# Linear attention before a GELU MLP: 64-token blocks from wave 2 on, earlier first scores, half loads and a last block in three pieces

## The chip, the cores and the metric

The kernel runs on one core of a Trainium2 chip. Its engines each work through a queue of their own in order: TensorE (matrix products into PSUM), VectorE, ScalarE, GpSimd, and SyncE (SP), which here issues nearly all DMAs. The metric is the time of one execution on the device in microseconds, as the median of several runs. In the profile TensorE is PE (its weight loads PEld), VectorE DVE, ScalarE ACT and GpSimd POOL.

## The reference

Inputs are `q`, `k`, `v` with 4 batches, 8 heads, 768 tokens and 64 columns per head, a decay `lam` per head, and two weight matrices of 512x2048 and 2048x512.

```
for each block of 64 tokens, each batch and head:
    scores = (q k^T) * lam^(i-j) for i >= j, else 0
    out    = scores v + (q * lam^(i+1)) state
    state  = lam^64 state + (k * lam^(63-j))^T v
x = out as 3072 tokens x 512 columns
h = x w_in                       # 3072 x 2048
y = (h * sigmoid(1.702 h)) w_out # 3072 x 512
```

The recurrence over blocks gives the same result for any block length, up to rounding; with blocks of 128 the decay of the state is `lam^128`.

## The kernel before

The 3072 tokens are worked through in six **waves** of 512. Waves 0 and 1 take the first 256 tokens of two batches each, by functions whose names begin with `big_`; they are not changed. Waves 2 to 5 take the next 128 tokens of all four batches. The eight heads are four **pairs** p, two heads side by side on the 128 partitions. Each wave consists of attention, which makes `xT` (512 columns of x by 512 tokens, transposed), and of the MLP: 16 steps `mlp1` of four 512-column matmuls with a GELU on ScalarE (L413 to L423), then 16 steps `mlp2` of four matmuls, four steps to an output tile g of 128 tokens, which VectorE copies out of PSUM and SP stores (L428 to L439).

The attention of wave w + 1 is spread through the MLP of wave w. The order is written out by hand: `main` is the list of MLP steps, `side` a list of (position, call), and a call is issued ahead of the step of its position (L546 to L569). Every engine's queue follows this order. For waves 2 to 5 the calls are:

- `load` (L76): 24 DMAs on SP's queue, for a wave two ahead.
- `do_cast` (L204) for each pair: four VectorE products make `kqs`, k and q in bfloat16 with their decays; GpSimd casts v (`v_sb`); a DMA transpose on SP's queue turns `kqs` into `kqT`.
- `scores` (L358) for two pairs: q k^T of 128 tokens by 128 for each batch and head, 16 matmuls on half the rows of the array, and four VectorE passes that multiply by decay and causal mask (`sm`).
- `mix` (L390) for two pairs: 8 matmuls of the state `kv_sb` with q (L395) and 16 of `v_sb` with `sm` (L402) into `ps_o`, which ScalarE casts to `xT`. It can carry the `scores` of the next two pairs, and the states of all pairs behind the last `mix` of a wave: `state_mm` (L373) makes k^T v in PSUM, `state_up` (L383) is one VectorE operation per head, new = old * lam^128 + k^T v.

PSUM has eight banks: three ("mm") serve the MLP's sums, five ("att") the attention; `scores` inside `mix` borrows one of the three (`bank`, L220). A new tile takes the bank whose last use came first in program order, and its first matmul waits until that use is over. The constants (`consts`, `last_consts`, `late_mask`, `state_zeros`) are made at the start. The last output tile of all is computed in two halves of 256 columns (`mlp2_part`, L441).

Of the kernel before, what the change touches and what calls it, by code (L numbers as in the profile page):

```python
# [24 lines left out]
def kernel(  # L25
# [50 lines left out]
    def load(w):  # L76
        for g in range(2):
# [44 lines left out]
    mask_b, mask = const.tile([P, 2, 2, D], bf16, name="mask_b"), const.tile([P, 1, P], bf16, name="mask")  # L122
# [3 lines left out]
    blk_pow = const.tile([P, NP], f32, name="blk_pow")  # L126

    def consts(f0):
# [5 lines left out]
        nc.gpsimd.iota(i_k, pattern=[[0, 1]], base=P - 1, channel_multiplier=-1, **io)  # L134
        nc.gpsimd.iota(i_q, pattern=[[0, 1]], base=1, channel_multiplier=1, **io)
        nc.vector.memset(i_inv, -float(P))
        nc.vector.memset(i_blk, float(P))
# [20 lines left out]
    def last_consts():  # L158
        for h in range(2):
# [5 lines left out]
    def late_mask():  # L165
        nc.gpsimd.affine_select(mask, mask, pattern=[[0, 1], [1, P]], channel_multiplier=-1, base=0,
                                compare_op=mybir.AluOpType.is_ge, fill=0.0)

    def state_zeros():
        for p in range(NP):  # L170
            for i in range(2):
                nc.gpsimd.memset(kv_sb[i][p], 0.0)

    v_sb = [[const.tile([P, G, 2, D], bf16, name=f"v_sb{i}{p}") for p in range(NP)] for i in range(2)]
    kv_sb = [[const.tile([P, B, P], bf16, name=f"kv{i}{p}") for p in range(NP)] for i in range(2)]
    part_sb = [[const.tile([P, 2, BB, D], f32, name=f"part{i}{r}") for r in range(2)] for i in range(2)]
# [134 lines left out]
    def big_st(w, p0):  # L311
        first, second = part_sb[p0 // 2]
        for i in range(2):
            p = p0 + i
            nc.gpsimd.tensor_scalar(first[:, i], first[:, i], scalar1=blk_pow[:, p : p + 1], scalar2=None, op0=MUL)  # L315
# [41 lines left out]

    def scores(w, pairs, spare=False):  # L358
        s2 = {(p, h): bank([P, B, P], f32, "ps_s", spare and (p, h) == (pairs[-1], 1)) for p in pairs for h in range(2)}
        for p in pairs:  # L360
            kq = trans[w, p]
            for b in range(B):
                for h in range(2):
                    hs = slice(64 * h, 64 * h + 64)
                    nc.tensor.matmul(s2[p, h][:, b, :], kq[hs, 0, b, :], kq[hs, 1, b, :], start=True, stop=True)  # L365
        for p in pairs:
            for h in range(2):
                sm = work.tile([P, B, P], bf16, tag="sm", bufs=8, name="sm")
                nc.vector.scalar_tensor_tensor(sm, s2[p, h], inv_pow[:, 2 * p + h : 2 * p + h + 1],  # L369
                                               mask.to_broadcast([P, B, P]), op0=MUL, op1=MUL)  # L370
                masked[w, p, h] = sm

    def state_mm(w, pairs):  # L373
        ps_kv = bank([P, len(pairs), B, D], f32, "ps_kv")
        for i, p in enumerate(pairs):
            ks, vt = cast[w, p][:, 0], v_sb[w % 2][p]
            for b in range(B):
                for h in range(2):
                    hs = slice(64 * h, 64 * h + 64)
                    nc.tensor.matmul(ps_kv[hs, i, b, :], ks[:, b, hs], vt[:, b, h, :], start=True, stop=True)  # L380
        return ps_kv

    def state_up(w, pairs, ps_kv):  # L383
        for i, p in enumerate(pairs):
            for h in range(2):
                hs = slice(64 * h, 64 * h + 64)
# [213 lines left out]
```

## Time and profile before

| | |
|---|---|
| runs shown | 216.71, 211.70, 212.51 us; median 212.51 |
| profiled execution | 211.42 us, its span (first to last instruction) 209.7 |
| TensorE busy | 200.8 us, 96% of the span |
| VectorE, ScalarE, GpSimd busy | 93.1, 86.8, 44.9 us |
| granted TensorE clock | full in all slices |

The profile is of one execution. "Span" runs from the first to the last instruction; the execution's own time has some 1.7 us around it. A timeline row gives the start in us from the span's start, the length in us, the engine, the line and operation, the tiles and the count of instructions merged in the row; what stands in brackets is idle time ahead of it and what ended it. A matmul's length is from its start until its result stands in PSUM; matmuls overlap, so that the spacing of starts is much shorter than a length.

### The profile page before, as it was taken

Reading aid. Unit: us, or ns where it says so; the run is one execution under the profiler, and the core shown is the slowest. Engines: PE = TensorE matmul, PEld = TensorE weight load, DVE = VectorE, ACT = ScalarE, POOL = GpSimd, SP = SyncE. Lnnn points to the kernel's source line nnn. Section 1 sums busy time; section 2 is a strip of 40 time slices with the busy share of each in tenths; the row PEclk is TensorE's granted clock in tenths of the full one; section 3 lists DMA queues with packets and bytes.
Section 4 is the critical chain, followed back from the end, with each engine's and each line's share of the span. In section 5 each row is a group of like instructions: output and inputs, shape, how many; then the busy total and the mean of one; then the engine's idle time right before and its main releaser. Section 6 shows DMA issues by size and latency. Waiting matters only on the chain.

```text
span 209.7 us, 4312 instructions
## 1 busy us (share of the span) xinstructions
PE 200.8 (96%) x1719; PEld 105.1 (50%) x1747; DVE 93.1 (44%) x199; ACT 86.8 (41%) x160; POOL 44.9 (21%) x87
## 2 busy tenths in 40 slices
PE   7979999998999999999999999999999999999993
PEld 7654444464444456444545444545444545444462
DVE  3895000578840568915347905346915341100121
ACT  4658662346765022565202566202466202565000
POOL 3299950174871011200211001120000000000000
PEclk9999999999999999999999999999999999999999
DMA  6999999998799999998891599890570111100112
GB/s 173 276 207 205 206 204 220 299 270 194 175 254 261 182 226 189 299 190 199 198 247 63 152 188 222 196 248 3 149 152 0 52 51 50 53 0 0 50 54 96
DMA packets 88233, 33.83 MB, mean 161 GB/s; under 512 B 68630, under 2 KB 85270, under 8 KB 88214
## 3 DMA queue, kind: packets, MB, share of 16 engines
q1 hardware_dynamic: 83174, 28.98, 58.2%
q0 software_dynamic: 4224, 4.19, 12.4%
q10 hardware_dynamic: 816, 0.39, 0.6%
q8 instruction: 13, 0.21, 0.4%
q14 instruction: 6, 0.05, 0.1%
HBM read 27.26 MB, written 6.29 MB: 160 GB/s over the span
## 4 chain that ended last, share of the span: by engine, by line
PE 89%; DVE 6%; DMA 2%; issue 2%; SPq 0%; ACT 0%; DVEq 0%
PE ps_h L420 39%; PE ps_out L433 38%; DVE smb L279 3%; PE ps_o L402 2%; PE ps_s L365 2%; DVE kqb L241 2%; PE ps_o L395 2%; PE ps_part L444 2%; DMA kb<-in_k_dram 2%; PE ps_s L271 1%; PE ps_kv L380 1%; PE ps_o L338 1%; DVE xT L349 1%; PE ps_tk L258 1%; PE ps_tq L258 0%
## 5 line engine op out<-in xcount | busy, mean ns | idle before, releaser
L420 PE MATMUL ps_h<-xT,w_in 128*128 128x512 bf16 x375 | 84.2, 379 | 0.7 <-issue 0.2
L433 PE MATMUL ps_out<-w_out,g_sb 128*128 128x512 bf16 x352 | 80.4, 379 | 1.8 <-issue 1.4
L423 ACT ACTIVATE g_sb<-ps_h 128x512 bf16<-128x512 f32 x96 | 57.0, 597 | 44.1 <-PE ps_h L420 44.0
L420 PEld LDWEIGHTS <-w_in 128*128 128x128 bf16 x384 | 37.1, 98 | 44.7 <-issue 0.3
L433 PEld LDWEIGHTS <-g_sb 128*128 128x128 bf16 x368 | 35.0, 98 | 41.0
L437 DVE COPY o_sb<-ps_out 128x512 f32<-128x512 f32 x19 | 12.9, 690 | 51.0 <-PE ps_out L433 50.4
L369 DVE SCALAR_TENSOR_TENSOR sm<-ps_s,inv_pow,mask 128x512 bf16<-128x512 f32 x32 | 21.8, 742 | 22.7 <-PE ps_s L365 22.7
L407 ACT CAST xT<-ps_o 128x512 bf16<-128x512 f32 x16 | 8.6, 589 | 42.9 <-PE ps_o L402 36.2
L213 POOL CAST v_sb<-vf 128x512 bf16<-128x512 f32 x16 | 9.9, 624 | 71.4 <-DMA vf<-in_v_dram 62.3
L387 DVE SCALAR_TENSOR_TENSOR kv<-kv,blk_pow,ps_kv 64x256 bf16<-64x256 bf16 x24 | 11.5, 480 | 7.6 <-PE ps_kv L380 6.9
L241 DVE TENSOR_TENSOR kqb<-kb,kb_pow 128x256 bf16<-128x256 f32 x10 | 4.0, 422 | 22.4 <-DMA kb<-in_k_dram 20.2
L210 DVE TENSOR_SCALAR kqs<-kf,k_pow 128x256 bf16<-128x256 f32 x32 | 12.1, 379 | 1.8 <-DMA kf<-in_k_dram 1.6
L211 DVE TENSOR_SCALAR kqs<-qf,q_pow 128x256 bf16<-128x256 f32 x32 | 11.5, 358 | 1.4 <-DMA qf<-in_q_dram 1.4
L279 DVE SCALAR_TENSOR_TENSOR smb<-ps_s,inv_pow,mask_b 128x512 bf16<-128x512 f32 x16 | 11.0, 745 | 2.3 <-PE ps_s L271 2.3
L318 POOL TENSOR_TENSOR kv<-part,part 64x128 bf16<-64x128 f32 x16 | 7.3, 456 | 1.2
L229 PE MATMUL fill<-warm 128*128 128x64 bf16 (+2 forms) x61 | 5.6, 272 | 1.2 <-DVE warm L105 1.2
L229 PEld LDWEIGHTS <-warm 128*128 128x128 bf16 x79 | 5.5, 124 | 2.0 <-DVE warm L105 1.2
L315 POOL TENSOR_SCALAR part<-part,blk_pow 128x128 f32<-128x128 f32 x8 | 5.4, 673 | 3.5 <-ACT part L309 2.9
L241 DVE TENSOR_TENSOR kqb<-qb,qb_pow 128x256 bf16<-128x256 f32 x13 | 6.0, 497 | 0.0
L437 ACT COPY o_sb<-ps_out 128x512 f32<-128x512 f32 x4 | 2.3, 585 | 8.3 <-PE ps_out L433 8.3
L258 PEld LDWEIGHTS <-kqb 128*128 128x128 bf16 x64 | 4.4, 103 | 1.9 <-DVE kqb L241 0.4
L395 PEld LDWEIGHTS <-kv 128*128 128x128 bf16 x64 | 4.2, 98 | 1.9
(70 smaller groups left out, 111.5 us busy)
## 6 DMA issues: line engine op xcount, KB each, us to landing
out_dram<-o_sb SPq DMA_DIRECT2D x23, 256.0 KB, 2.6
kf<-in_k_dram SPq DMA_DIRECT2D x32, 128.0 KB, 3.3
qf<-in_q_dram SPq DMA_DIRECT2D x32, 128.0 KB, 3.5
vf<-in_v_dram SPq DMA_DIRECT2D x32, 128.0 KB, 3.3
vb<-in_v_dram SPq DMA_DIRECT2D x8, 256.0 KB, 5.0
w_in<-in_moe_w_in_dram POOLq DMA_DIRECT2D x4, 512.0 KB, 9.5
w_out<-in_moe_w_out_dram POOLq DMA_DIRECT2D x4, 512.0 KB, 16.5
kb<-in_k_dram SPq DMA_DIRECT2D x8, 128.0 KB, 3.6
```

The costliest lines, as they stand in the source:

```text
L210: nc.vector.tensor_scalar(ks[:, :, h, :], kf[:, :, h, :], scalar1=k_pow[:, hd : hd + 1], scalar2=None, op0=MUL)
L211: nc.vector.tensor_scalar(qs[:, :, h, :], qf[:, :, h, :], scalar1=q_pow[:, hd : hd + 1], scalar2=None, op0=MUL)
L213: nc.gpsimd.tensor_copy(v_sb[w % 2][p], vf)
L229: nc.tensor.matmul(dst, warm[:, :P], warm[:, : dst.shape[1]], start=True, stop=True, skip_group_check=True)
L241: eng.tensor_tensor(x[:, bb].rearrange("p t (h d) -> p h t d", h=2), pair_of(w, nm, p)[:, bb], by, op=MUL)
L279: nc.vector.scalar_tensor_tensor(sm.rearrange("p b t s -> p b (t s)"), s2.rearrange("p b t s -> p b (t s)"), inv_pow[:, 2 * p + h : 2 * p ...
L369: nc.vector.scalar_tensor_tensor(sm, s2[p, h], inv_pow[:, 2 * p + h : 2 * p + h + 1], mask.to_broadcast([P, B, P]), op0=MUL, op1=MUL)
L387: nc.vector.scalar_tensor_tensor(kv_sb[(w + 1) % 2][p][hs, :, hs], kv_sb[w % 2][p][hs, :, hs], blk_pow[hs, p : p + 1], ps_kv[hs, i], op0=M ...
L420: nc.tensor.matmul(h_ps[fc], w_in_sb[j][:, kc, i * P : (i + 1) * P], xT[w, kc], start=(kc == 0), stop=(kc == KC - 1))
L423: nc.scalar.activation(g_of[w][:, fc, :], h_ps.pop(fc), GELU)
L433: nc.tensor.matmul(ps_out, g_of[w][:, fc, g * P : (g + 1) * P], w_out_sb[j][:, fc % CW, :], start=(fc == 0), stop=(fc == FFC - 1))
L437: (nc.scalar.copy if w == 0 else nc.vector.tensor_copy)(o, ps_out)
```

## The change

From wave 2 on, each wave's 128 tokens are two blocks r = 0, 1 of 64. `scores` makes only the two 64x64 blocks on the diagonal, as 32 matmuls of 64x64 weights for two pairs, one for each of the four quarters of the array; the mask is one VectorE product for each head index over two pairs with a precomputed float32 table `mask_pow` (decay and causal mask together). `state_mm` makes k^T v for each block apart, and `state_up` goes in two steps: `half_sb` = `kv_sb` * lam^64 + first block, new `kv_sb` = `half_sb` * lam^64 + second block; in wave 5 the first step alone. `mix` uses `kv_sb` for the first block and `half_sb` for the second (L412 of the new kernel, 64 columns each) and needs the state update of its own wave, which `attend` or the part `then` of a `mix` brings just before. `then` now makes scores and states of the named wave.

In the MLP of wave 2 the last `mix` carries the first scores and states of wave 4, in that of wave 3 those of wave 5; the first two casts of these waves move ahead accordingly, to steps 15 and 16.5, and their loads are issued in two halves. Other positions shift with them. The zeroing of `kv_sb[1]` and `half_sb` moves to steps 8 and 16 of wave 0, the small tables are made on GpSimd in `late_pows`. The last output tile comes in pieces of 256, 128 and 128 columns.

```diff
-    def load(w):
-        for g in range(2):
+    def load(w, gs=(0, 1)):
+        for g in gs:
...
     def last_consts():
+        for x, i in ((l64, i_blk), (k_pow, i_k), (q_pow, i_q)):
+            nc.scalar.activation(x, ln_lam, EXP, scale=i)
...
+    def late_pows():
         for h in range(2):
             hs = slice(64 * h, 64 * h + 64)
-            nc.scalar.activation(blk_pow[hs], ln_lam[hs].rearrange("p (n h) -> p n h", h=2)[:, :, h], EXP, scale=i_blk[hs])
-        for x, i in ((k_pow, i_k), (q_pow, i_q)):
-            nc.scalar.activation(x, ln_lam, EXP, scale=i)
...
+            nc.gpsimd.tensor_copy(blk_pow[hs], l64[hs].rearrange("p (n h) -> p n h", h=2)[:, :, h])
+        nc.gpsimd.tensor_tensor(blk2_pow, blk_pow, blk_pow, op=MUL)
+        nc.gpsimd.tensor_tensor(l64, l64, inv_pow, op=MUL)
+        nc.gpsimd.tensor_tensor(mask_pow.rearrange("p n h s -> p (n h) s"), mask[:, None, :].to_broadcast([P, H, D]),
+                                l64[:, :, None].to_broadcast([P, H, D]), op=MUL)
...
+    quads = [(r, slice(64 * r, 64 * r + 64), h, slice(64 * h, 64 * h + 64)) for r in range(2) for h in range(2)]
+
     def scores(w, pairs, spare=False):
-        s2 = {(p, h): bank([P, B, P], f32, "ps_s", spare and (p, h) == (pairs[-1], 1)) for p in pairs for h in range(2)}
-        for p in pairs:
+        s2 = [bank([P, 2, B, D], f32, "ps_s", spare and h == 0) for h in range(2)]
+        for i, p in enumerate(pairs):
             kq = trans[w, p]
             for b in range(B):
-                for h in range(2):
-                    hs = slice(64 * h, 64 * h + 64)
-                    nc.tensor.matmul(s2[p, h][:, b, :], kq[hs, 0, b, :], kq[hs, 1, b, :], start=True, stop=True)
-        for p in pairs:
-            for h in range(2):
-                sm = work.tile([P, B, P], bf16, tag="sm", bufs=8, name="sm")
-                nc.vector.scalar_tensor_tensor(sm, s2[p, h], inv_pow[:, 2 * p + h : 2 * p + h + 1],
-                                               mask.to_broadcast([P, B, P]), op0=MUL, op1=MUL)
-                masked[w, p, h] = sm
+                for r, rs, h, hs in quads:
+                    nc.tensor.matmul(s2[h][rs, i, b, :], kq[hs, 0, b, rs], kq[hs, 1, b, rs], start=True, stop=True)
+        for h in range(2):
+            sm = work.tile([P, 2, B, D], bf16, tag="sm", bufs=8, name="sm")
+            nc.vector.tensor_tensor(sm, s2[h], mask_pow[:, pairs[0] : pairs[0] + 2, h, None, :].to_broadcast([P, 2, B, D]),
+                                    op=MUL)
+            masked[w, pairs[0], h] = sm
 
     def state_mm(w, pairs):
-        ps_kv = bank([P, len(pairs), B, D], f32, "ps_kv")
+        nr = 2 if w + 1 < NW else 1
+        ps_kv = [bank([P, 2, B, D], f32, f"ps_kv{r}") for r in range(nr)]
...
+                for r, rs, h, hs in quads[: 2 * nr]:
+                    nc.tensor.matmul(ps_kv[r][hs, i, b, :], ks[rs, b, hs], vt[rs, b, h, :], start=True, stop=True)
+        return ps_kv
+
+    def state_up(w, pairs, ps_kv):
+        for r, kv in enumerate(ps_kv):
+            for i, p in enumerate(pairs):
+                old, new = (kv_sb[w % 2][p], half_sb[p]) if r == 0 else (half_sb[p], kv_sb[(w + 1) % 2][p])
...
+                    nc.vector.scalar_tensor_tensor(new[hs, :, hs], old[hs, :, hs], blk_pow[hs, p : p + 1], kv[hs, i],
+                                                   op0=MUL, op1=ADD)
+
+    def attend(w, pairs):
+        scores(w, pairs)
+        state_up(w, pairs, state_mm(w, pairs))
+
+    def mix(w, pairs, then=()):
+        ps_o = [bank([P, 2, B, D], f32, f"ps_o{r}") for r in range(2)]
         for i, p in enumerate(pairs):
...
+            for r in range(2):
+                kv = half_sb[p] if r else kv_sb[w % 2][p]
+                for b in range(B):
+                    nc.tensor.matmul(ps_o[r][:, i, b, :], kv[:, b, :], trans[w, p][:, 1, b, r * D : r * D + D],
+                                     start=(i == 0 and b == 0), stop=False, skip_group_check=True)
+        for i, p in enumerate(pairs):
             vt = v_sb[w % 2][p]
             for b in range(B):
...
+                for r, rs, h, hs in quads:
+                    nc.tensor.matmul(ps_o[r][hs, i, b, :], vt[rs, b, h, :], masked[w, pairs[0], h][rs, i, b, :],
                                      start=False, stop=True, skip_group_check=True)
...
+        x = x_tile(w, pairs[0]).rearrange("p i (b r s) -> p r (i b) s", b=B, r=2)
+        for r in range(2):
+            nc.scalar.copy(x[:, r], ps_o[r].rearrange("p i b s -> p (i b) s"))
         if then:
-            scores(w, then, True)
-        for ps2, kv in zip(states, ps_kv):
-            state_up(w, ps2, kv)
+            scores(*then, True)
+            state_up(*then, state_mm(*then))
...
-                    + [(mlp2_part, w, G - 1, c0, d_model // 2) for c0 in (0, d_model // 2)])
+                    + [(mlp2_part, w, G - 1, c0, n) for c0, n in ((0, 2 * P), (2 * P, P), (3 * P, P))])
...
-                side += [(n + 1 + 2.0 * p, (do_cast, w + 1, p)) for p in range(NP)]
-                all_pairs, at = ([0, 1], [2, 3]), (21, 25, 28) if w == 1 else (13, 20, 27)
-                side += [(n + at[0], (scores, w + 1, [0, 1])), (n + at[1], (mix, w + 1, [0, 1], (), [2, 3])),
-                         (n + at[2], (mix, w + 1, [2, 3], all_pairs if w + 2 < NW else ()))]
-            if w and w + 2 < NW:
-                side += [(n + 8, (load, w + 2))]
+                ahead = w > 1 and w + 2 < NW
+                p0 = 2 if w > 2 else 0
+                side += [(n + 1 + 2.0 * (p - p0), (do_cast, w + 1, p)) for p in range(p0, NP)]
+                if w < 3:
+                    side += [(n + (21 if w == 1 else 13), (attend, w + 1, [0, 1]))]
+                side += [(n + (25 if w == 1 else 18 if w == 2 else 13), (mix, w + 1, [0, 1], (w + 1, [2, 3]))),
+                         (n + (28 if w == 1 else 27), (mix, w + 1, [2, 3], (w + 2, [0, 1]) if ahead else ()))]
+                if w == 1:
+                    side += [(n + 8, (load, w + 2))]
+                if ahead:
+                    side += [(n + (8 if w == 2 else 5), (load, w + 2, (0,))), (n + 21, (load, w + 2, (1,)))]
+                    side += [(n + 15 + 1.5 * p, (do_cast, w + 2, p)) for p in range(2)]
```

More of the change, by code (lines that the diff above doesn't have):

```diff
@@ L121 @@
     i_inv, i_blk = const.tile([P, 1], f32, name="i_inv"), const.tile([P, 1], f32, name="i_blk")
[L122 removed]
+    mask_b, mask = const.tile([P, 2, 2, D], bf16, name="mask_b"), const.tile([P, D], f32, name="mask")
     ln_lam = const.tile([P, H], f32)
@@ L125 @@
     inv_pow, k_pow, q_pow = (const.tile([P, H], f32, name=f"{x}_pow") for x in ("inv", "k", "q"))
-    blk_pow = const.tile([P, NP], f32, name="blk_pow")
+    l64 = const.tile([P, H], f32, name="l64")
+    blk_pow, blk2_pow = (const.tile([P, NP], f32, name=f"{x}_pow") for x in ("blk", "blk2"))
+    mask_pow = const.tile([P, NP, 2, D], f32, name="mask_pow")
     def consts(f0):
@@ L398, in mix @@
             vt = v_sb[w % 2][p]
             for b in range(B):
-                for h in range(2):
-                    hs = slice(64 * h, 64 * h + 64)
-                    nc.tensor.matmul(ps_o[p][hs, b, :], vt[:, b, h, :], masked[w, p, h][:, b, :],
+                for r, rs, h, hs in quads:
+                    nc.tensor.matmul(ps_o[r][hs, i, b, :], vt[rs, b, h, :], masked[w, pairs[0], h][rs, i, b, :],
                                      start=False, stop=True, skip_group_check=True)
-        ps_kv = [state_mm(w, ps2) for ps2 in states]
```

47 lines of the change are left out of this document (16 added, 31 removed).

## The prediction

> **What bounds the kernel now.** I read the page first: busy times, the slices, the chain that ended last, and two of its costliest groups (count | busy us, mean ns | idle before).
>
> ```profile
> span 209.7 us, 4312 instructions
> ...
> PE 200.8 (96%) x1719; PEld 105.1 (50%) x1747; DVE 93.1 (44%) x199; ACT 86.8 (41%) x160; POOL 44.9 (21%) x87
> ...
> POOL 3299950174871011200211001120000000000000
> ...
> PE 89%; DVE 6%; DMA 2%; issue 2%; SPq 0%; ACT 0%; DVEq 0%
> ...
> L433 PE MATMUL ps_out<-w_out,g_sb 128*128 128x512 bf16 x352 | 80.4, 379 | 1.8 <-issue 1.4
> ...
> L369 DVE SCALAR_TENSOR_TENSOR sm<-ps_s,inv_pow,mask 128x512 bf16<-128x512 f32 x32 | 21.8, 742 | 22.7 <-PE ps_s L365 22.7
> ```
>
> TensorE is busy 96% of the span and holds 89% of the chain. So behind the start the time is the sum of what is put on TensorE's queue, and a change counts by what it takes off that queue, by the waits it puts into it, and by what it does to the end. The profiled execution took 211.42 us (span 209.7); the median shown is 212.51, 1.1 above it.
>
> Next the timeline of TensorE in the MLP of wave 1, which holds the attention of wave 2 (start, length, line, count):
>
> ```profile
> 66.40 4.48 PE L433 MATMUL ps_out<-w_out,g_sb 128*128 128x512 bf16 x20
> ...
> 70.81 0.62 PE L365 MATMUL ps_s<-kqT 64*128 64x128 bf16 x16
> ...
> 71.37 3.63 PE L433 MATMUL ps_out<-w_out,g_sb 128*128 128x512 bf16 x15
> ...
> 74.83 0.61 PE L395 MATMUL ps_o<-kqT,kv 128*128 128x128 bf16 x8
> ...
> 75.37 0.64 PE L402 MATMUL ps_o<-sm,v_sb 128*64 128x128 bf16 x16
> ...
> 75.94 0.62 PE L365 MATMUL ps_s<-kqT 64*128 64x128 bf16 x16
> ...
> 76.72 2.54 PE L433 MATMUL ps_out<-w_out,g_sb 128*128 128x512 bf16 x11 [0.16 <-issue]
> ...
> 80.11 0.67 PE L380 MATMUL ps_kv<-v_sb,kqs 128*64 128x64 bf16 x32
> ...
> 80.94 3.40 PE L433 MATMUL ps_out<-w_out,g_sb 128*128 128x512 bf16 x15 [0.16 <-issue]
> ```
>
> A 512-column matmul follows the last by (4.48 - 0.379) / 19 = 0.216 us, so four make an MLP step of 0.863 us. What a block of attention costs is what lies between the last MLP start before it and the first after it, less 0.216. The run at 66.40 has its last start at 66.40 + 4.48 - 0.379 = 70.50; the next is at 71.37: the scores alone cost 0.65. In the same way outputs plus scores cost 76.72 - 74.62 - 0.216 = 1.89, and outputs plus states 80.94 - 78.88 - 0.216 = 1.84. Waves 3 and 4 repeat this. Wave 5 has no state to make:
>
> ```profile
> 167.16 5.99 PE L433 MATMUL ps_out<-w_out,g_sb 128*128 128x512 bf16 x27 [0.16 <-issue]
> ...
> 174.32 1.03 PE L433 MATMUL ps_out<-w_out,g_sb 128*128 128x512 bf16 x4 [0.16 <-issue]
> ```
>
> 174.32 - 172.77 - 0.216 = 1.34. Together 3 x (0.65 + 1.89 + 1.84) + (0.65 + 1.89 + 1.34) = **17.0 us** of TensorE, the part that the change rewrites. The groups of matmuls by form give one matmul's length:
>
> ```profile
> L395 PE MATMUL ps_o<-kqT,kv 128*128 128x128 bf16 x64 | 4.9, 219 | 0.0
> ...
> L380 PE MATMUL ps_kv<-v_sb,kqs 128*64 128x64 bf16 x96 | 2.0, 196 | 0.0
> ```
>
> The group at 74.83 makes eight steps of (0.61 - 0.219) / 7 = 0.056, that is 0.45, and so do the two groups of pairs behind it. The outputs alone (1.34) are 0.90 of steps and 0.44 of switching between array shapes and back; with scores behind them (1.89) it is 1.34 and 0.55.
>
> **The change, part by part.** *New matmuls.* Scores, masked outputs and states become groups of 32 matmuls of 64x64 with 64 columns, four at once. Waves 0 and 1 already have that form in L298:
>
> ```profile
> 42.39 1.03 PE L433 MATMUL ps_out<-w_out,g_sb 128*128 128x512 bf16 x4
> 43.34 0.64 PE L271 MATMUL ps_s<-kqB 64*64 64x128 bf16 x32
> 43.81 0.48 PE L298 MATMUL ps_kv<-vb,kqb 64*64 64x64 bf16 x32
> 44.45 1.67 PE L433 MATMUL ps_out<-w_out,g_sb 128*128 128x512 bf16 x7 [0.16 <-issue]
> ```
>
> The pairs of L380 give (0.67 - 0.196) / 15 = 0.0317 for a step of 64 columns; L298's 32 matmuls are eight steps, 0.25 (its 0.48 less one matmul is 0.28 for seven: its second half came 0.06 late). The whole stretch costs 44.45 - 43.04 - 0.216 = 1.19; with 64 instead of 128 columns in its first half (0.45 to 0.25) and without that wait it is **0.95**, my price of scores plus states standing alone (`attend`).
>
> *Outputs from the state.* Eight 128x128 loads with 128 columns become sixteen with 64 (L412 of the new kernel). No row has this form at the warm pace. From below: half of 0.056, 0.028; from above the early fills, the only 128x128 loads with 64 columns:
>
> ```profile
> L229 PE MATMUL fill<-warm 128*128 128x64 bf16 x40 | 2.3, 242 | 0.0
> ```
>
> (2.3 - 0.24) / 39 = 0.053 each. I take 0.0317, the pace of the warm 64-column rows of L380, because the wide load is not the longer one:
>
> ```profile
> L395 PEld LDWEIGHTS <-kv 128*128 128x128 bf16 x64 | 4.2, 98 | 1.9
> ...
> L380 PEld LDWEIGHTS <-kqs 128*64 128x64 bf16 x96 | 1.8, 113 | 0.0
> ```
>
> 98 ns for 128 columns, 113 for 64. The Trainium skill, page "TensorE: Matmul & The Clock Gate", section "LDWEIGHTS (loading the stationary operand)", speaks against this: a load takes its columns over 1.2, 107 ns for 128, which its section on Fast Weight Load halves. By that halved figure the sum below would be some 2 us higher; what such a pace does here is the first rival. The two rows above do not grow with the columns as that rule has it.
>
> Scores and states now have the shape of the outputs in front of them, so no switch is added: outputs plus scores plus states cost 16 x 0.0317 + 3 x 0.25 + 0.44 = **1.70**, outputs alone 0.51 + 0.25 + 0.44 = **1.20**. The calls are: in wave 1's MLP 0.95 + 1.70 + 1.20, in wave 2's 0.95 + 1.70 + 1.70, in wave 3's 1.70 + 1.70 (wave 5 makes only its first half state, in pairs, the same eight steps), in wave 4's 1.70 + 1.20. Sum 14.5: **TensorE gains 2.5 us**, between 3.0 (0.028) and -0.2 (0.053).
>
> *VectorE.* Its rows in wave 2:
>
> ```profile
> 103.64 2.73 DVE L369 SCALAR_TENSOR_TENSOR sm<-ps_s,inv_pow,mask 128x512 bf16<-128x512 f32 x4 [0.65 <-PE ps_s L365]
> 107.43 0.69 DVE L437 COPY o_sb<-ps_out 128x512 f32<-128x512 f32 x1 [1.06 <-PE ps_out L433]
> 111.29 4.07 DVE L387 SCALAR_TENSOR_TENSOR kv<-kv,blk_pow,ps_kv 64x256 bf16<-64x256 bf16 x8 [3.17 <-PE ps_kv L380]
> 115.39 1.29 DVE L437 COPY o_sb<-ps_out 128x512 f32<-128x512 f32 x2
> 116.71 0.35 DVE L210 TENSOR_SCALAR kqs<-kf,k_pow 128x256 bf16<-128x256 f32 x1
> 116.98 0.35 DVE L211 TENSOR_SCALAR kqs<-qf,q_pow 128x256 bf16<-128x256 f32 x1
> ```
>
> A mask pass takes 0.68 (2.73 / 4), a state update 0.51 (4.07 / 8), an output copy 0.60 to 0.69, a cast 0.27. For two head pairs four mask passes become two, but four state updates become eight: 2.7 + 2.0 becomes 1.4 + 4.1 = 5.5 us. The new mask is a product with a float32 table; I take the 0.68 of the same size out of PSUM (from below 0.60, the second copy of 115.39; from above the group's 742 ns, no overlap). These 5.5 us now stand between scores and outputs, in one queue with the output copies, whose banks TensorE needs. Worked through in program order, on the clock of the rows above:
>
> Wave 1's MLP: scores at 70.81, masks from 71.3 to 72.65, half states to 74.7, new states to 76.75. (From the last matmul of a group to VectorE I allow 0.25: the 0.196 of that matmul and a little.) TensorE leaves the block 0.3 later than before, does four steps and starts the outputs at 75.1; at 76.2 (0.51 + 0.25 + 0.25 and a switch later) it wants the second state bank, which is free at 76.75: **wait 0.55**. Then VectorE has an output copy (77.4), masks (78.7) and half states (80.8); TensorE does three steps from 77.3 and wants the last half state at 80.3: **wait 0.5**.
>
> Wave 2's end: let t be the end of wave 4's first scores. VectorE is done with masks and states at t + 0.25 + 5.45 = t + 5.7 and with the copy queued behind them at t + 6.4. TensorE has the states (0.25), the way back (0.3) and six steps, 5.7, until the second step of wave 3, which needs that copy's bank: **wait 0.7**. Scores of wave 5 have half the updates, so wave 3's end waits for nothing, and outputs in waves 3 and 4 come 12 steps behind their states. Waits: **1.75 us**; with 0.60 and 0.74 for a mask 1.3 to 2.1.
>
> *Loads and casts.* In wave 2 the casts of wave 4's first two pairs move up to step 15, in front of the masks of wave 3, and wait in VectorE's queue for the first half load. Queued behind them are the masks and states of wave 3's second pairs and two output copies. The queue of SP:
>
> ```profile
> 86.66 6.37 SPq L216 DMA_TRANSPOSE kqT<-kqs  x4
> 93.09 1.15 SPq L83 DMA_DIRECT2D kf<-in_k_dram  x2
> ...
> 97.58 2.28 SPq L83 DMA_DIRECT2D qf<-in_q_dram  x2
> ```
>
> ```profile
> DMA to landing us min/median/max: 2.9/3.0/4.2
> ```
>
> A pair of loads takes 1.15 to issue, a transpose 1.6; 97.58 stalled for about 1.1. The tenth load, the last needed, has left at 97.58 + 2.28 = 99.9, by the first wait above 0.5 later, and lands 3.0 to 4.2 after that, 103.4 to 104.6; VectorE asks at about 103.4. From the first scores to the bank freed by the first output copy VectorE has 5.5 + 2.1 + 5.5 + 0.7 = 13.8 us of work and TensorE 14 steps and 3.2 of blocks, 15.3, so some 1.3 is spare; I count nothing, and up to 1.5 if a second stall falls here. The transposes follow at about 104 to 107 and are wanted 5 us later. The second half load stands in front of three output stores, which have four buffers and nobody waiting; its casts fall in wave 3's first steps, where VectorE is free, ten steps ahead of use. In wave 3 the first half load leaves behind two transposes and is wanted 10 us later; its transposes land some 2 us before the scores.
>
> *GpSimd and ScalarE.* Zeroing moves to steps 8 and 16 of wave 0 and one table product is new: behind its first state work (slices of 5.2 us) the POOL digits are 5, 0 and 1, until 42 us, and nobody waits. ScalarE's output casts keep size and number (now written in runs of 64), with four steps until the next wave reads them: nothing.
>
> *The end.*
>
> ```profile
> 202.59 3.66 PE L444 MATMUL ps_part<-w_out,g_sb 128*128 128x256 bf16 x32
> ...
> 206.29 0.42 DVE L447 COPY o_part<-ps_part 128x256 f32<-128x256 f32 x1 [1.32 <-PE ps_part L444]
> ```
>
> ```profile
> out_dram<-o_sb SPq DMA_DIRECT2D x23, 256.0 KB, 2.6
> ...
> out_dram<-o_part SPq DMA_DIRECT2D x2, 128.0 KB, 1.7
> ```
>
> The last copy has 128 columns instead of 256: 0.69 for 512 and 0.42 for 256 make 0.29, a gain of 0.13. The last store is halved; 2.6 and 1.7 for 256 and 128 KB allow 0 to 0.45, I take 0.15. TensorE pays 32 x 0.056 + 16 x 0.109 against 32 x 0.109, 0.04 more. **End: -0.25.**
>
> **Sum:** -2.5 + 1.75 - 0.25 = **-1.0 us**: 210.4 beside the profiled execution, 211.5 beside the median. I take the middle, 211.0.
>
> **The rivals.** *Weight loads set the pace of L412.* For it: the fills' 0.053. Against: 98 against 113 ns. Over 8 x 16 matmuls it adds 128 x 0.0213 = 2.7, and gives back some 0.6 of the waits, since TensorE arrives later: 213.1. It turns the change into a loss from 0.040 us a matmul on. *VectorE becomes the bound in wave 2.* For it: 13.8 us of queue with about 1.3 spare, behind a load that lands just in time. Updates of 0.57 instead of 0.51 lengthen each of the three waits by 8 x 0.06, 1.4 in all, and use up the spare; a half load that lands 2 us late adds 0.7 to 2: 212 to 214.5. Against: the durations come from rows of the same form. It is a loss from 1.0 us of added wait on. *The waits are not there* (shorter masks and updates, or more slack than I see): 211.0 - 1.75 = 209.3.
>
> **How the numbers follow.** Forecast (209.9 to 212.0) 0.58; weight loads (212.4 to 213.6) 0.12; VectorE (212 to 214.5) 0.18; no waits (208.8 to 209.9) 0.12. The range 209.2 to 213.8 leaves out a third of the last and of VectorE's case, and little else. Two per cent, 4.2 us, is about what the measurement can tell from no change. Faster by that needs more than the whole gain without a wait, 0.03; slower needs both slow rivals together, 0.06; the rest is 0.91.
>
> **What would show it.** In the profile of the changed kernel: 16 L412 matmuls spaced 0.03 (not 0.05) apart; 32-matmul groups of 0.44 length each; 56 state updates, 0.51 apart; TensorE waiting for VectorE three times, about half a us each, in wave 1's MLP and at the start of wave 3; no wait for a transposed tile. A wait for a state or an output bank of over 1 us in wave 2, or L412 at 0.05, would make the forecast wrong.

## The result and the profile after

The changed kernel takes 210.93 us (median of 20 runs, 210.21 to 212.38); the kernel before, run beside it, 212.25 (median of 20, 211.18 to 216.71). The ratio is 0.9959, with a 95% interval of 0.994 to 0.9979: faster by 0.87 us, between 0.45 and 1.27, well inside the two per cent that I called no change. The ratio is of fast runs alone; four of the 20 runs of the kernel before were slow (214.9 us and more), so that the medians lie further apart, by 1.32. I had said 211.0, and -1.0 us.

The page of the changed kernel's profiled execution (212.38 us), with the lines that answer to those of before. What were L420, L433 and L369 are L434, L447 and L379; L399 is the state update.

```profile
span 210.7 us, 5246 instructions
...
PE 200.4 (95%) x2183; PEld 105.1 (50%) x2211; DVE 96.7 (46%) x216; ACT 86.9 (41%) x159; POOL 49.1 (23%) x99
...
PE 78%; DMA 7%; DVE 5%; SPq 4%; issue 2%; ACT 2%; ACTq 0%; POOL 0%; POOLq 0%
...
L447 PE MATMUL ps_out<-w_out,g_sb 128*128 128x512 bf16 x355 | 80.4, 379 | 1.6 <-issue 1.3
...
L379 DVE TENSOR_TENSOR sm<-ps_s,mask_pow 128x512 bf16<-128x512 f32 x16 | 10.3, 686 | 29.1 <-PE ps_s L376 29.1
L399 DVE SCALAR_TENSOR_TENSOR half<-kv,blk_pow,ps_kv 64x256 bf16<-64x256 bf16 x32 | 15.3, 478 | 0.7
...
L399 DVE SCALAR_TENSOR_TENSOR kv<-half,blk_pow,ps_kv 64x256 bf16<-64x256 bf16 x24 | 11.5, 480 | 0.8
```

TensorE still bounds the kernel (95% busy). Its share of the chain that ended last fell from 89% to 78%; loads rose from 2% to 7% and the queue of SP from 0% to 4%, while VectorE has 5% after 6%. A second pair of traces (below) has TensorE at 89% and 81% and VectorE at 0% and 7%: VectorE's masks and states now stand on the chain in places. VectorE has 16 mask passes instead of 32, and 56 state updates instead of 24.

This execution is 1 us *longer* than the profiled one of before, though the medians say the opposite. The first MLP matmul tells why. First the row of before, then that of the changed kernel (timeline of TensorE):

```profile
18.09 5.22 PE L420 MATMUL ps_h<-xT,w_in 128*128 128x512 bf16 x22
```

```profile
19.93 3.24 PE L434 MATMUL ps_h<-xT,w_in 128*128 128x512 bf16 x13
```

1.8 us are lost before the attention that the change rewrites has begun. Two further profiles, of the same two kernels and unchanged, put the two starts at 18.96 and 19.08. So I compare stretches inside the traces, and the ratio of the times for the whole.

The further traces showed a second thing, and it concerns my own working. The matmuls of line L433 in the second trace of the kernel before (groups by line; count | busy, mean ns | idle ahead):

```profile
L433 PE MATMUL ps_out<-w_out,g_sb 128*128 128x512 bf16 x368 | 82.8, 379 | 0.0
```

The row that I quoted ahead of the prediction had x352: 16 of 368 records were missing. The timeline of the second trace in wave 1's MLP:

```profile
71.50 0.62 PE L365 MATMUL ps_s<-kqT 64*128 64x128 bf16 x16
72.05 3.63 PE L433 MATMUL ps_out<-w_out,g_sb 128*128 128x512 bf16 x16
75.51 0.61 PE L395 MATMUL ps_o<-kqT,kv 128*128 128x128 bf16 x8
76.05 0.64 PE L402 MATMUL ps_o<-sm,v_sb 128*64 128x128 bf16 x16
76.62 0.62 PE L365 MATMUL ps_s<-kqT 64*128 64x128 bf16 x16
77.18 2.76 PE L433 MATMUL ps_out<-w_out,g_sb 128*128 128x512 bf16 x12
...
80.79 0.67 PE L380 MATMUL ps_kv<-v_sb,kqs 128*64 128x64 bf16 x32
81.39 2.98 PE L433 MATMUL ps_out<-w_out,g_sb 128*128 128x512 bf16 x13
```

Three steps are 12 matmuls, and here there are 12; in the row of 76.72 that I quoted there were 11, with "[0.16 <-issue]" at its end. The record of the first matmul behind the block was missing, and its 0.216 went into my price of the block. By the complete trace outputs plus scores cost 77.18 - (72.05 + 3.63 - 0.379) - 0.216 = 1.66 and not 1.89, outputs plus states 1.61 and not 1.84. The scores alone stay at 0.65, since there the missing record lay further back. No time was lost where records are missing. The second half of wave 5's MLP, in the first and in the second trace:

```profile
192.23 10.52 PE L433 MATMUL ps_out<-w_out,g_sb 128*128 128x512 bf16 x47
```

```profile
192.91 10.52 PE L433 MATMUL ps_out<-w_out,g_sb 128*128 128x512 bf16 x48
```

From wave 2's first scores to there it is 192.23 - 70.81 = 121.42 us in the first trace and 192.91 - 71.50 = 121.41 in the second.

The same stretch in the second trace of the changed kernel:

```profile
68.73 3.19 PE L447 MATMUL ps_out<-w_out,g_sb 128*128 128x512 bf16 x14
71.84 0.45 PE L376 MATMUL ps_s<-kqT 64*64 64x64 bf16 x32
...
72.51 3.63 PE L447 MATMUL ps_out<-w_out,g_sb 128*128 128x512 bf16 x16
75.97 0.28 PE L412 MATMUL ps_o<-kqT,kv 128*128 128x64 bf16 x4
76.09 0.28 PE L412 MATMUL ps_o<-kqT,half 128*128 128x64 bf16 x4
76.21 0.28 PE L412 MATMUL ps_o<-kqT,kv 128*128 128x64 bf16 x4
76.32 0.28 PE L412 MATMUL ps_o<-kqT,half 128*128 128x64 bf16 x4
76.53 0.44 PE L418 MATMUL ps_o<-sm,v_sb 64*64 64x64 bf16 x32
...
77.12 0.22 PE L390 MATMUL ps_kv<-v_sb,kqs 64*64 64x64 bf16 x2
77.72 0.44 PE L390 MATMUL ps_kv<-v_sb,kqs 64*64 64x64 bf16 x30 [0.38 <-DVE kv L399]
78.09 2.76 PE L447 MATMUL ps_out<-w_out,g_sb 128*128 128x512 bf16 x12
...
81.69 0.29 PE L412 MATMUL ps_o<-kqT,half 128*128 128x64 bf16 x4 [0.48 <-DVE half L399]
...
82.28 3.63 PE L447 MATMUL ps_out<-w_out,g_sb 128*128 128x512 bf16 x16
...
192.63 10.52 PE L447 MATMUL ps_out<-w_out,g_sb 128*128 128x512 bf16 x48
```

`attend` costs 72.51 - 71.54 - 0.216 = 0.76, the first outputs with scores and states 78.09 - 75.76 - 0.216 = 2.11, the second outputs 82.28 - 80.47 - 0.216 = 1.59 (1.60 in the first trace). All blocks of waves 2 to 5, read in this way from complete traces (where the trace of a run lacks the record behind a block, one 0.216 slot and a little more, 0.227, is taken off):

| us of TensorE | before | changed | said for the change |
|---|---|---|---|
| wave 1's MLP | 0.65 + 1.66 + 1.61 | 0.76 + 2.11 + 1.60 | 0.95 + 1.70 + 1.20, waits 0.55 + 0.5 |
| wave 2's | 0.65 + 1.66 + 1.61 | 0.76 + 1.57 + 1.57, then a wait of 0.67 | 0.95 + 1.70 + 1.70, wait 0.7 |
| wave 3's | 0.65 + 1.66 + 1.61 | 1.56 + 1.49 | 1.70 + 1.70 |
| wave 4's | 0.65 + 1.66 + 1.11 | 1.54 + 0.94 | 1.70 + 1.20 |
| sum | 15.2 | 14.6 (12.7 + waits 1.9) | 16.3 against 17.0 |

The blocks gain 0.6, and the end 0.2: from the start of the last whole block's last matmul to the end of the span 210.3 - 203.06 = 7.24 becomes 209.8 - 202.77 = 7.03. Together -0.8, where the times say -0.87. The whole stretch from wave 2's first scores to the second half of wave 5's MLP bears out the sums without any single block: it is 192.63 - 71.84 = 120.79 in this trace and 193.50 - 72.73 = 120.77 in the first one of the changed kernel, 0.62 to 0.65 less than before.

The waits are in the list of what TensorE waited for (second trace of the changed kernel; total, times, longest):

```profile
PE ps_h L434 <- DVE o_sb L451: 0.5, 1, 0.5
PE ps_o L412 <- DVE half L399: 0.5, 1, 0.5
...
PE ps_kv L390 <- DVE kv L399: 0.4, 1, 0.4
```

No such line stood in the list of before. A wait costs more than its row: idle time is counted from the modelled end of the last matmul, 0.195 us after its start at 64 columns and 0.379 at 512, while the next would have followed after 0.03 or 0.216. So 0.38 in the timeline is 0.38 + 0.195 - 0.03 = 0.54 (measured as 2.11 - 1.57 = 0.54), 0.48 is 0.64 (measured as 1.60 - 0.94 = 0.66), 0.51 is 0.67. The Trainium skill, page "Perfetto Trace Analysis", section "Tensor Engine Instruction (MATMUL, LD_WEIGHTS)", says that the end of a TensorE record is a model and not a measurement; these three waits agree.

### The profile page after: what moved, and what is told of

It reads as the page before. It is cut to its first block, busy times and chain, and to the rows that moved or that the text cites. A ratio compares the mean times of both kernels' runs of the same rounds, so it can differ in the third digit from the quotient of the medians.

```text
span 210.7 us, 5246 instructions
## 1 busy us (share of the span) xinstructions
PE 200.4 (95%) x2183; PEld 105.1 (50%) x2211; DVE 96.7 (46%) x216; ACT 86.9 (41%) x159; POOL 49.1 (23%) x99
## 3 DMA queue, kind: packets, MB, share of 16 engines
q0 software_dynamic: 4224, 4.19, 12.2%
## 4 chain that ended last, share of the span: by engine, by line
PE 78%; DMA 7%; DVE 5%; SPq 4%; issue 2%; ACT 2%; ACTq 0%; POOL 0%; POOLq 0%
PE ps_h L434 38%; PE ps_out L447 31%; DMA vb<-in_v_dram 3%; SPq L83 2%; DMA qb<-in_q_dram 2%; DVE half L399 2%; SPq L96 2%; PE ps_part L458 2%; DVE kv L399 2%; PE ps_o L412 1%; PE ps_o L418 1%; DMA qf<-in_q_dram 1%; DVE sm L379 1%; PE ps_s L376 1%; PE ps_kv L390 1%
## 5 line engine op out<-in xcount | busy, mean ns | idle before, releaser
L434 PE MATMUL ps_h<-xT,w_in 128*128 128x512 bf16 x372 | 84.3, 379 | 1.3 <-DVE o_sb L451 0.5
L447 PE MATMUL ps_out<-w_out,g_sb 128*128 128x512 bf16 x355 | 80.4, 379 | 1.6 <-issue 1.3
L434 PEld LDWEIGHTS <-w_in 128*128 128x128 bf16 x384 | 36.9, 98 | 45.3 <-issue 1.1
L447 PEld LDWEIGHTS <-g_sb 128*128 128x128 bf16 x368 | 35.1, 98 | 41.0
L379 DVE TENSOR_TENSOR sm<-ps_s,mask_pow 128x512 bf16<-128x512 f32 x16 | 10.3, 686 | 29.1 <-PE ps_s L376 29.1
L399 DVE SCALAR_TENSOR_TENSOR half<-kv,blk_pow,ps_kv 64x256 bf16<-64x256 bf16 x32 | 15.3, 478 | 0.7
L221 DVE TENSOR_SCALAR kqs<-qf,q_pow 128x256 bf16<-128x256 f32 x32 | 12.5, 390 | 0.3 <-DMA qf<-in_q_dram 0.3
L220 DVE TENSOR_SCALAR kqs<-kf,k_pow 128x256 bf16<-128x256 f32 x32 | 12.2, 383 | 0.2
L399 DVE SCALAR_TENSOR_TENSOR kv<-half,blk_pow,ps_kv 64x256 bf16<-64x256 bf16 x24 | 11.5, 480 | 0.8
L239 PEld LDWEIGHTS <-warm 128*128 128x128 bf16 x79 | 6.0, 130 | 2.0 <-DVE warm L105 1.2
L251 DVE TENSOR_TENSOR kqb<-qb,qb_pow 128x256 bf16<-128x256 f32 x13 | 5.3, 450 | 0.0
```

What stands on the lines that cost most here:

```text
L220: nc.vector.tensor_scalar(ks[:, :, h, :], kf[:, :, h, :], scalar1=k_pow[:, hd : hd + 1], scalar2=None, op0=MUL)
L221: nc.vector.tensor_scalar(qs[:, :, h, :], qf[:, :, h, :], scalar1=q_pow[:, hd : hd + 1], scalar2=None, op0=MUL)
L239: nc.tensor.matmul(dst, warm[:, :P], warm[:, : dst.shape[1]], start=True, stop=True, skip_group_check=True)
L251: eng.tensor_tensor(x[:, bb].rearrange("p t (h d) -> p h t d", h=2), pair_of(w, nm, p)[:, bb], by, op=MUL)
L379: nc.vector.tensor_tensor(sm, s2[h], mask_pow[:, pairs[0] : pairs[0] + 2, h, None, :].to_broadcast([P, 2, B, D]), op=MUL)
L399: nc.vector.scalar_tensor_tensor(new[hs, :, hs], old[hs, :, hs], blk_pow[hs, p : p + 1], kv[hs, i], op0=MUL, op1=ADD)
```

## The experiments

**The end alone.** The kernel before with the last block in three pieces.

```diff
-  + [(mlp2_part, w, G - 1, c0, d_model // 2) for c0 in (0, d_model // 2)]
+  + [(mlp2_part, w, G - 1, c0, n) for c0, n in ((0, 2 * P), (2 * P, P), (3 * P, P))]
```

> The kernel before with one part of the change alone: the last block in three pieces. My theory prices this at -0.25 us (the two traces give -0.23 from the last whole block to the end), so a ratio to the kernel before of 0.9988 and, in its profile, 7.05 instead of 7.29 us from the last block's first matmul to the end of the span. The rival, that the last store is what ends the program and does not shrink with its size, gives -0.1 us (0.9995). It is also a second look at the start of the kernel before: its first MLP matmul started at 18.1 us, that of the changed kernel at 19.9. If that difference is only how the first loads fell, this run may as well show 19 to 20; if the change itself delays the start, it shows 18.1 again.

Ratio 1.0005 (0.9973 to 1.0037): the time can tell neither value. The trace gives 210.8 - 203.75 = 7.05 us, as forecast. The start was at 19.65, so the kernel before starts late too.

**Blocks of 64 alone.** The first scores of waves 4 and 5 stand alone again, behind whole loads.

```diff
-  ahead = w > 1 and w + 2 < NW
-  p0 = 2 if w > 2 else 0
+  ahead = False
+  p0 = 0
...
-  if w < 3:
-      side += [(n + (21 if w == 1 else 13), (attend, w + 1, [0, 1]))]
-  side += [(n + (25 if w == 1 else 18 if w == 2 else 13), (mix, w + 1, [0, 1], (w + 1, [2, 3]))),
+  side += [(n + (21 if w == 1 else 13), (attend, w + 1, [0, 1]))]
+  side += [(n + (25 if w == 1 else 20), (mix, w + 1, [0, 1], (w + 1, [2, 3]))),
...
-  if w == 1:
+  if w + 2 < NW:
       side += [(n + 8, (load, w + 2))]
```

> The changed kernel with the second and third part undone: the first scores of waves 4 and 5 stand alone at step 13, as wave 3's do, behind whole loads at step 8. My theory: each of the two blocks costs 0.95 alone where it cost about 0.50 behind an output step, +0.9 together, and the wait at the start of wave 3 (0.68 in the trace) goes, since the last output step of wave 2 has no states behind it: +0.2 us against the changed kernel, a ratio to the kernel before of 0.997. The rival, that the early casts and half loads of wave 2 do more harm than the saved switches do good: -0.5 us against the changed kernel or less, 0.994 and below.

Ratio 0.9938 (0.9902 to 0.9973), and the blocks cost 14.1 in its trace: 0.45 less than in the changed kernel, not 0.2 more. My forecast was wrong here, and the size is the one that the rival had named. The wait at the start of wave 3 went, as I had said. But the two blocks standing alone cost only 0.13 and 0.17 more than behind an output step (0.76 against 1.57 - 0.94 = 0.63, and 0.72 against 1.49 - 0.94 = 0.55), not 0.45. The price of the block alone was wrong because of the missing records, 0.95 was 0.76; and behind an output the same groups cost 0.63 and 0.55, not 0.50. So by the traces the second and third parts of the change (earlier scores, half loads) together cost more than they save as they are placed; the times alone, with intervals that overlap, do not show it. The rival's reason, early casts and half loads, did not show: no wait of TensorE for them stands in either trace.

**The output copies on ScalarE.**

```diff
-  (nc.scalar.copy if w == 0 else nc.vector.tensor_copy)(o, ps_out)
+  (nc.scalar.copy if w < NW - 1 else nc.vector.tensor_copy)(o, ps_out)
```

> The changed kernel with the output copies of waves 1 to 4 on ScalarE instead of VectorE (ScalarE does wave 0's already, 0.59 us each, and has no GELU to do in those steps). My theory, that the waits of TensorE come from the length of VectorE's queue: the wait at the start of wave 3 (0.68) goes, and so does the wait for the last half state in wave 1 (0.48), since the copy of 0.69 us in front of the masks is gone; the wait for the state bank (0.38) stays, as no copy stands in front of it. Against the changed kernel -1.1 us, ratio to the kernel before 0.991. The rival, that these waits are hidden behind something else (a load, a bank, ScalarE's own queue): 0 to -0.4 us, 0.995.

Ratio 0.9881 (0.9829 to 0.9934). Of the three waits that the change brought, one is left, the first of these rows:

```profile
PE ps_kv L390 <- DVE kv L399: 0.4, 1, 0.4
PE ps_o L337 <- ACT mid L315: 0.4, 1, 0.4
```

The second row belongs to wave 1's attention, which is not changed; the kernel before has it too, as L327. The last half state and the start of wave 3 are free, and the blocks cost 13.3, which is 1.3 less than in the changed kernel. The state bank's block still costs 2.11, as forecast.

**Two blocks moved**, with VectorE's work as it was.

```diff
-  (n + (28 if w == 1 else 27), (mix, w + 1, [2, 3], (w + 2, [0, 1]) if ahead else ()))
+  (n + (29 if w == 1 else 25 if w == 2 else 27), (mix, w + 1, [2, 3], (w + 2, [0, 1]) if ahead else ()))
```

> The changed kernel with two blocks moved: the second outputs of wave 2 one step later (step 29 of wave 1's MLP instead of 28), the second outputs of wave 3 two steps earlier (25 instead of 27). VectorE does the same work in the same order. My theory: the wait for the last half state (0.48) goes, since one more step gives 0.86 us; the wait for the output copy at the start of wave 3 (0.68) goes, since the states are done 1.7 us earlier. Against the changed kernel -1.1 us, ratio to the kernel before 0.991. The rival, that the moved blocks meet their own inputs late (casts of the outputs on ScalarE behind step 29, transposed tiles of wave 4 at step 25): at or above the changed kernel, 0.996 to 0.999.

Ratio 0.9926 (0.989 to 0.9963), blocks 13.9: 0.7 less, not 1.1. Both waits went, but the block moved to step 25 met a new one:

```profile
PE ps_s L376 <- DVE o_sb L451: 0.6, 1, 0.6
```

The scores inside `mix` borrow a bank of the MLP's three. At step 25 the bank that they get was still held by an output tile whose copy waited in VectorE's queue behind masks and states; the block cost 2.22 instead of 1.57. Neither theory had named that.

**VectorE's queue, priced.** Every mask pass of waves 2 to 4 twice.

```diff
+  if w in (2, 3, 4):
+      nc.vector.tensor_tensor(sm, s2[h], mask_pow[:, pairs[0] : pairs[0] + 2, h, None, :].to_broadcast([P, 2, B, D]),
+                              op=MUL)
   masked[w, pairs[0], h] = sm
```

> The changed kernel with every mask pass of waves 2 to 4 done twice: VectorE gets 2 x 0.6 = 1.2 us more for each pair group, all else is the same. This measures what VectorE's queue costs TensorE. My theory, that in wave 1's MLP VectorE works without a pause from the first scores to the last half state, so that the waits there grow by the whole of both added pairs of passes (2.4), and that at the start of wave 3 the wait grows by 1.2 at the least, and by as much as 2.4 if the spare in wave 2 is used up: +3.6 to +4.9 us against the changed kernel, a ratio to the kernel before of 1.013 to 1.019. In waves 3 and 4 (twelve steps between states and use) nothing. The rival, that VectorE has room everywhere but at the three places, and each of the waits grows by less than one added pair of passes: under +2.5 us, below 1.008.

Ratio 1.0213 (1.0163 to 1.0263), 5.4 us above the changed kernel's 0.9959, somewhat over the upper forecast. The profiled execution was 3 us longer than the median, nearly all of them lost before the first MLP matmul (22.23), so I read only its blocks. VectorE in wave 1's MLP (L382 is the added pass, L402 the state update):

```profile
75.39 0.69 DVE L379 TENSOR_TENSOR sm<-ps_s,mask_pow 128x512 bf16<-128x512 f32 x1 [0.57 <-PE ps_s L376]
76.12 0.69 DVE L382 TENSOR_TENSOR sm<-ps_s,mask_pow 128x512 bf16<-128x512 f32 x1
76.73 0.68 DVE L379 TENSOR_TENSOR sm<-ps_s,mask_pow 128x512 bf16<-128x512 f32 x1
77.44 0.69 DVE L382 TENSOR_TENSOR sm<-ps_s,mask_pow 128x512 bf16<-128x512 f32 x1
78.05 2.00 DVE L402 SCALAR_TENSOR_TENSOR half<-kv,blk_pow,ps_kv 64x256 bf16<-64x256 bf16 x4
```

An added pair of passes took 78.05 - 75.39 - 1.20 = 1.46, and not the 1.2 that I had added (a pass that repeats the one before it on the same tiles follows it by 0.71 to 0.73, not 0.60). In wave 1's MLP the blocks grew from 2.11 + 1.60 to 3.56 + 3.05, by 2.9, the whole of two such pairs. In wave 2's, with three pairs (4.4), the blocks and the waits at the start of wave 3 grew by 2.7 (0.76 + 2.64 + 2.54 + 1.35 against 0.76 + 1.57 + 1.57 + 0.67): there 1.7 us lay beside other work, where I had reckoned with "some 1.3" of spare. Most of this growth, 2.0, is inside wave 2's two later blocks, where TensorE now waits for a state bank and for an output's bank; I had put it at the start of wave 3 alone. In waves 3 and 4 nothing grew (1.55, 1.49, 1.54, 0.94).

**The two kernels again, unchanged**, for complete traces.

> The kernel before, unchanged, for a second trace. Its first trace has 16 fewer records of the second MLP matmuls than there are matmuls, the run with the last block in three pieces has all of them. Where one is missing right behind a block of attention, the block seems 0.22 us dearer than it is. I expect blocks of 0.65, 1.66 and 1.61 (1.11 in wave 5), 15.2 us together, and not the 17.0 that I summed; the rival, that they cost 1.89 and 1.84 and the other run was cheaper because of its own change, gives 17.0 again. Its first MLP matmul may start anywhere from 18 to 20 us.

> The changed kernel, unchanged, for a second trace: with all records I expect blocks and the wait at the start of wave 3 of 14.6 us together (16.2 in its first trace), waits of 0.54, 0.66 and 0.68 among them, and 0.6 less than the same sum of the kernel before. Its first MLP matmul may start anywhere from 18 to 20 us.

15.2 and 14.6, as expected; these are the tables and rows above.

**Copies on ScalarE, by the line shown above, and later outputs in wave 1's MLP.**

```diff
-  side += [(n + (25 if w == 1 else 18 if w == 2 else 13), (mix, w + 1, [0, 1], (w + 1, [2, 3]))),
-           (n + (28 if w == 1 else 27), (mix, w + 1, [2, 3], (w + 2, [0, 1]) if ahead else ()))]
+  side += [(n + (26 if w == 1 else 18 if w == 2 else 13), (mix, w + 1, [0, 1], (w + 1, [2, 3]))),
+           (n + (29 if w == 1 else 27), (mix, w + 1, [2, 3], (w + 2, [0, 1]) if ahead else ()))]
```

> The changed kernel with the output copies of waves 1 to 4 on ScalarE, as in the earlier run, and in wave 1's MLP the outputs of wave 2 one step later each (steps 26 and 29 instead of 25 and 28). With the copies alone one wait of the three was left, for the state bank, in a block that cost 2.11 where the same block in wave 2 costs 1.57. My theory: one step (0.86) more between the first states and the first outputs takes that wait too (0.54), nothing new is late, and the blocks cost 12.7 to 12.8 us together, 2.5 less than before; with the end that is -2.7 us, a ratio to the kernel before of 0.987. The rival, that the later block meets a new wait (the masks behind it, or the casts of the outputs before wave 2): no faster than with the copies alone.

209.59 us, ratio 0.9868 (0.982 to 0.9916), faster than both kernels (the changed kernel's interval begins at 0.994). The blocks are at 12.9, said 12.7 to 12.8; wave 1's part of the timeline:

```profile
73.71 4.49 PE L447 MATMUL ps_out<-w_out,g_sb 128*128 128x512 bf16 x20
78.04 0.28 PE L412 MATMUL ps_o<-kqT,kv 128*128 128x64 bf16 x4
...
79.61 2.76 PE L447 MATMUL ps_out<-w_out,g_sb 128*128 128x512 bf16 x12
82.21 0.28 PE L412 MATMUL ps_o<-kqT,kv 128*128 128x64 bf16 x4
...
82.72 0.29 PE L412 MATMUL ps_o<-kqT,half 128*128 128x64 bf16 x4
...
83.31 2.76 PE L447 MATMUL ps_out<-w_out,g_sb 128*128 128x512 bf16 x12
```

The block of 78.04 costs 1.57 now. That of 82.21 costs 1.10 instead of 0.94: the half state is late by 0.16.

**The same with the second outputs at step 30.**

```diff
-           (n + (29 if w == 1 else 27), ...
+           (n + (30 if w == 1 else 27), ...
```

> The fastest version so far (copies on ScalarE, outputs of wave 2 at steps 26 and 29), with the second of them at step 30. At 29 the block still cost 1.10 against 0.94 for the same block in wave 5, a rest of the wait for the last half state of 0.16. My theory: one step later this goes, -0.16 us by the trace, which the times can't tell (ratio 0.986 to 0.987). The rival: wave 2's first MLP steps, now two steps behind, wait for ScalarE's casts of these outputs (two of 0.59 behind the block, and before the GELU), up to +0.5 us, and the trace shows a wait of the first MLP for an ScalarE cast.

The rest of the wait went (0.94, blocks 12.7), and no wait of the MLP for a cast appeared. Ratio 0.9895 (0.9852 to 0.9937): the times cannot tell it from the version before.

**The control.** The kernel before with the copies of waves 1 to 4 on ScalarE, the same one-line edit.

> The kernel before with only the output copies of waves 1 to 4 moved to ScalarE, the control for the two runs of the changed kernel that have them there. My theory: in the kernel before no wait of TensorE ends on VectorE behind the start, so freeing VectorE buys nothing: ratio 1.000, blocks of attention of 15.2 us together as in its own trace. The rival, that ScalarE makes the copies cheaper for everybody (its 0.59 against 0.69 us, or stores that leave earlier): -1 us, 0.995.

Ratio 1.0011 (0.9982 to 1.004): nothing. Its trace lacks the same records as the first one of before, and after the same 0.227 for each of eight blocks the sum is 15.2. Its list of waits shows how such a hole looks:

```profile
PE ps_out L433 <- issue: 1.4, 9, 0.2
```

Nine "waits for issue" of 0.16, and 16 records missing from L433: by the two stretches of 121.4 us above there was no wait, only no record.

## Why the prediction was right

**TensorE's gain, said 2.5, was 15.2 - 12.7 = 2.5**, but both sides of it were wrong. Before was 15.2 and not 17.0, the new blocks without waits 12.7 and not 14.5. The step that failed is the price of a block, "what lies between the last MLP start before it and the first after it, less 0.216": it takes for granted that the record of the first start is there. Eight blocks of before carried 0.227 too much; my new prices were built on "0.44 of switching", which held the same 0.227 (it is 0.21), and on L298's stretch, which held it too. In the price of a single block alone against one behind an output the errors did not cancel, and the forecast for the blocks of 64 alone missed by 0.65. In the whole they did, and that is luck: the old blocks held the 0.227 eight times, my ten prices of new ones ten times, so that with this alone put right the gain would be 15.2 - 12.2 = 3.0. The other 0.5 is in the groups of 32 matmuls, which I priced at 0.25: behind an output they start 0.28 and 0.31 after the group in front of them (76.53, 76.81 and 77.12 above), and an output with scores and states costs 1.57, where the steps and 0.21 make 1.47. The count x352, against 368 that the code issues, was in the first fence of the prediction.

**Weight loads** do not set the pace. The rows of the changed kernel above have four groups of four starting 0.115 apart, 0.029 us a matmul, near the lower bound. The page "TensorE: Matmul & The Clock Gate" of the Trainium skill, section "LDWEIGHTS (loading the stationary operand)", has 107 ns for such a load, and its section "Weight-path perf modes — Fast Weight Load (FWL) and DoubleRow" about half of that; estimated from the halved figure, the sixteen would take 0.85 one behind the other, and they take 0.46. The rival falls.

**VectorE's price** was within its bounds: a mask pass follows the last by 1.29 - 0.69 = 0.60, the lower bound and not the 0.68 that I took, an update by 0.51 as taken. **The three waits** were where I had put them: 0.54, 0.66 and 0.67 by the blocks, 1.9, against 0.55, 0.5 and 0.7, 1.75. Their size is in part luck too, since for a mask of 0.60 the prediction itself gives 1.3. Against that, TensorE came sooner, as its blocks are cheaper: it wanted the second state bank 77.72 - 0.54 - 71.84 = 5.34 after the first scores began, where I had 76.2 - 70.81 = 5.39, and the last half state 81.69 - 0.64 - 77.72 = 3.33 after that bank came free, where I had 80.3 - 76.75 = 3.55. And VectorE began its first masks 0.56 behind the start of the scores (at 72.40), where I had 0.49.

The runs show that the waits come from VectorE's queue: two of them go when its copies go and the third with one step more between states and use, they grow by all that is added in front of them in wave 1's MLP, and the same copies removed from the kernel before, which has no such wait, give nothing. The rival without waits falls with that.

**VectorE in wave 2** was not the bound. In the changed kernel it still idles there, 0.79 ahead of the last masks (timeline of VectorE, second trace):

```profile
105.44 1.29 DVE L379 TENSOR_TENSOR sm<-ps_s,mask_pow 128x512 bf16<-128x512 f32 x2
106.64 2.01 DVE L399 SCALAR_TENSOR_TENSOR half<-kv,blk_pow,ps_kv 64x256 bf16<-64x256 bf16 x4
108.69 2.02 DVE L399 SCALAR_TENSOR_TENSOR kv<-half,blk_pow,ps_kv 64x256 bf16<-64x256 bf16 x4
110.74 1.29 DVE L451 COPY o_sb<-ps_out 128x512 f32<-128x512 f32 x2
112.82 1.29 DVE L379 TENSOR_TENSOR sm<-ps_s,mask_pow 128x512 bf16<-128x512 f32 x2 [0.79 <-PE ps_s L376]
```

With 4.4 added, 2.7 of it reached TensorE, so the spare there was some 1.7; I had put it at 1.3 (the figures that I gave for it, 15.3 and 13.8, differ by 1.5).

**The end** gave 0.23 and 0.21 in the two pairs of traces, said 0.25: the last copy is 0.29 as worked out, the store is a little less.

**The sum** was -2.5 + 1.75 - 0.25 = -1.0; by the traces it is -2.5 + 1.9 - 0.2 = -0.8, by the times -0.87. That 210.93 lies so near 211.0 is luck, as 211.0 was only the middle between 210.4 and 211.5. What I left out is the start: from the first instruction to the first MLP matmul the four traces of the kernel before and of its two versions took 18.1 to 19.7, seven of the changed kernel and its versions (the doubled masks left out) 18.6 to 20.4. That these come out 0.7 later on average may be chance; it was not settled. The new tables on GpSimd are not the reason: in the two traces of the changed kernel they are made from 23.2 and 22.3 us on, behind the first MLP matmul (19.93 and 19.08). The times leave little room for a later start: with 0.7 of it the gain would be 0.1, and it is 0.45 to 1.27.

## What to carry to other kernels

Before a stretch is priced from starts, compare the count of records with what the code issues; a short "issue" idle right behind a group, with one matmul too few in the row, is a missing record and not a cost. A change that takes work off the bounding engine by handing more steps to another is worth what the new queue leaves of it: here three waits took back 1.9 of 2.5, and moving one unrelated kind of work (output copies) to a third engine, with one step more between states and their use, gave back nearly all. Ahead of moving a block earlier, ask for every buffer that it borrows, too.

## What the runs showed of the hardware that I had not expected

- Going from 512-column matmuls to outputs in other array shapes and back costs 1.11 - 0.90 = 0.21 us in the kernel before, half of what I had read.
- A VectorE mask pass that repeats the one before it, on the same tiles, starts 0.71 to 0.73 us after it; one on other tiles starts 0.60 after it.
- Two traces of one and the same kernel reach their first MLP matmul 0.9 us apart (18.09 and 18.96; 19.93 and 19.08), and traces of versions whose start is the same lie within 1.6 to 1.8. What TensorE waits for last in front of it differs: in two traces of the kernel before and its versions it is the load of `w_in` (0.7 and 1.3), in both of the changed kernel the cast of `vb` on GpSimd. A single pair of traces can hide a gain of 0.9 behind that.
